# TensorE in two 64-row halves, the lower one lagging behind the upper, in the attention pairs 19 to 47

## The chip, the cores and the metric

The kernel runs on one core of a Trainium2 chip. The metric is the device time of one execution in microseconds. Three runs of the kernel before gave 401.55, 402.24 and 403.20 us; the median, 402.24 us, is the time before. The profile is of one execution of its own, with a span of 399.5 us from the first to the last instruction.

## The reference

Cosine attention is followed by a two-layer feed-forward block:

```python
q_n = q / (np.linalg.norm(q, axis=-1, keepdims=True) + 1e-06)      # q, k, v: 8 x 12 x 448 x 64
k_n = k / (np.linalg.norm(k, axis=-1, keepdims=True) + 1e-06)
scores = np.matmul(q_n, k_n.transpose(0, 1, 3, 2)) / tau
attn = softmax(scores)                                             # over the keys
x = (attn @ v).transpose(0, 2, 1, 3).reshape(3584, 768)
h = x @ w_in                                                       # 768 x 2048
g = h * np.clip(h + 3.0, 0.0, 6.0) / 6.0
out = g @ w_out                                                    # 2048 x 768
```

There are 8 batches of 12 heads, 448 tokens and 64 channels a head, in float32 in and out.

## The kernel before

The 96 heads are handled as 48 pairs, six pairs to a batch. Everything that TensorE multiplies is bf16, and everything it adds up lies in PSUM: two banks for the value products (PV, one for each head of a pair) and a ring of six banks (M0, M1, Y, Z, M2, M3) for all the rest.

For a pair, the queries and keys are loaded (`load_qk`), squared (`square`), reduced (`reduce`), turned into reciprocal norms on ScalarE (`norms`), normalised on GpSimd (`normalise`), transposed by a DMA (`crossbar`) into a tile tT, and the keys are copied into kz (`copy_k`) and km (`copy_k3`). Scores are computed with the keys on the partitions, in four groups. Groups 0 to 2 hold 128 keys of each head; the two heads lie on different 64 rows of TensorE's array, since a head has 64 channels. Group 3, "M", holds the last 64 keys of both heads in one matmul over all 128 rows, with the other quarters of km at zero. Each of the seven results takes a bank, and ScalarE turns it into exponentials (`exps`, L463) in a tile at. `values` (L486) multiplies them with the values, which have a column of ones, so that column 64 is the softmax's sum: 24 matmuls over 128 rows (groups 0 to 2) and 8 over 64 rows (group 3, four a head). `finish_values` (L506, L507) divides on VectorE, and `back_crossbar` or `back_two` transposes the result by a DMA into xT, of which there are two, one a batch.

The first layer (`mm1_unit`, L598) makes 128 of the 2048 features for a batch's 448 tokens with six matmuls of 448 columns in one bank. ScalarE makes the clipped factor (`relu`, L614) and VectorE the product g (L620); then the bank is free. `mm1_two` weaves two such units, so that the last of six matmuls of both comes at the end. The second layer works on pairs of 128-token blocks in Strassen-like form with seven products (`product_unit`, L794), named 1 to 7, eight matmuls of 384 columns each. VectorE makes the sums of g that they need (`g_sum`, L772). Products 2, 4, 5 and 3 are copied out by ScalarE (L813, L831, L842), products 1, 6 and 7 are added by VectorE (L819, L851), and GpSimd adds the parts up (L823 to L835). Products 6, 2 and 5 go on in the bank of 1, 4 and 3, after that bank was read, unless they are written as "5a" or "2a", with a bank of their own and an addition on GpSimd.

The order of the work is written out by hand. PLAN lists everything up to pair 17; then a loop makes one turn for each of the pairs 18 to 47, with the units of both layers that TURNS names for it (F is one first-layer unit, FF two woven ones, "4.3" product 4 of block pair 3, "+1.3" the sum for it) and sums on VectorE that `side` names. Instructions reach each engine's queue in this order and are executed in it. A turn of the kernel before starts with value group 3 of the pair before (64-row halves), the scores of groups 0 to 2 (64-row halves, in pairs), their exponentials, value groups 1 and 2 of the pair before, and its finish; then the units, with score group 3 behind the first; last, value group 0. After pair 47 the units of units[NP] finish the second half of the work without attention.

The functions that the change touches, and those that call them, with the profile's line numbers:

## Time and profile before

| | |
|---|---|
| median of three runs | 402.24 us (401.55 to 403.20) |
| profiled execution, span | 399.5 us |
| TensorE busy in the span | 391.4 us |
| VectorE, ScalarE, GpSimd busy | 291.1, 274.3, 235.9 us |
| granted TensorE clock, mean | 0.999 |
| turns 19 to 47, to the last value product (120.6 to 336.0 us) | 215.4 us |
| VectorE, ScalarE, GpSimd busy in them | 154.6, 154.6, 146.1 us |

The profile is a trace of every engine's instructions with their start and length, and of the semaphores that they wait for. Busy time is the union of an engine's instructions. A matmul's length is the time until its result is written, so that matmuls that follow each other closely overlap; the pace of TensorE is read from starts, not from lengths. "64*128" in a row is the rows and columns of the array that an instruction uses. A row of groups gives line, engine, operation, out<-in, shapes and count, then busy time and the mean length in ns, then the engine's idle time before it and what ended that.

### The profile page before, as it was taken

Reading aid. Unit: us, or ns where it says so; the run is one execution under the profiler, and the core shown is the slowest. Engines: PE = TensorE matmul, PEld = TensorE weight load, DVE = VectorE, ACT = ScalarE, POOL = GpSimd, SP = SyncE. Lnnn points to the kernel's source line nnn. Section 1 sums busy time; section 2 is a strip of 40 time slices with the busy share of each in tenths; the row PEclk is TensorE's granted clock in tenths of the full one; section 3 lists DMA queues with packets and bytes.
Section 4 is the critical chain, followed back from the end, with each engine's and each line's share of the span. In section 5 each row is a group of like instructions: output and inputs, shape, how many; then the busy total and the mean of one; then the engine's idle time right before and its main releaser. Section 6 shows DMA issues by size and latency. Waiting matters only on the chain.

```text
span 399.5 us, 9623 instructions
## 1 busy us (share of the span) xinstructions
PE 391.4 (98%) x3673; PEld 230.9 (58%) x3673; DVE 291.1 (73%) x514; ACT 274.3 (69%) x627; POOL 235.9 (59%) x234
## 2 busy tenths in 40 slices
PE   7999999999999999999999999999999999999996
PEld 5656466555555556555555555555565556555563
DVE  6898988889878597766878775976766565645663
ACT  6899998886887676887776776767658655224230
POOL 7897229652853989579859829688396500400070
PEclk9999999999999999999999999999999999999999
DMA  8999987797987678795888386694953424230133
GB/s 292 291 226 252 240 188 206 149 172 193 222 201 171 159 193 183 174 231 152 196 178 230 81 203 158 155 198 136 193 125 75 103 48 67 46 74 21 31 71 97
DMA packets 92365, 63.73 MB, mean 160 GB/s; under 512 B 56096, under 2 KB 91552, under 8 KB 92320
## 3 DMA queue, kind: packets, MB, share of 16 engines
q1 hardware_dynamic: 87408, 56.45, 58.6%
q0 software_dynamic: 4512, 6.29, 9.3%
q8 instruction: 28, 0.46, 0.5%
q10 hardware_dynamic: 400, 0.39, 0.3%
q14 instruction: 17, 0.14, 0.1%
HBM read 45.61 MB, written 11.01 MB: 142 GB/s over the span
## 4 chain that ended last, share of the span: by engine, by line
PE 90%; ACT 5%; DMA 1%; DVE 1%; POOL 1%; issue 0%; SPq 0%; ACTq 0%
PE M L598 24%; PE M L794 19%; PE PV L486 11%; PE Y L598 6%; PE Z L598 6%; PE M L445 5%; PE Z L794 5%; PE Y L794 4%; ACT at L463 4%; PE Z L445 1%; PE Y L445 1%; PE M L874 1%; PE PV L1016 1%; DMA big<-in_q_dram 1%; POOL nrm L297 1%; PE Z L659 1%
## 5 line engine op out<-in xcount | busy, mean ns | idle before, releaser
L598 PE MATMUL M<-xT,w_in_sb 128*128 128x448 bf16 x522 | 110.7, 353 | 0.1
L598 PEld LDWEIGHTS <-w_in_sb 128*128 128x128 bf16 x768 | 72.0, 98 | 62.2 <-issue 1.9
L463 ACT ACTIVATE at<-M 128x448 bf16<-128x448 f32 x192 | 96.4, 569 | 16.7 <-PE M L445 15.7
L297 POOL TENSOR_TENSOR nrm<-big,r 128x896 bf16<-128x896 f32 (+1 forms) x46 | 77.1, 1680 | 27.8 <-ACT r L260 10.7
L229 POOL TENSOR_TENSOR big<-big 128x896 f32<-128x896 f32 (+3 forms) x41 | 60.8, 1488 | 16.6 <-DVE n L241 11.0
L620 DVE SCALAR_TENSOR_TENSOR gT<-u,M 128x448 bf16<-128x448 bf16 x76 | 46.2, 616 | 32.0 <-ACT u L614 31.8
L614 ACT ACTIVATE u<-M 128x448 bf16<-128x448 f32 x87 | 48.5, 560 | 28.3 <-PE M L598 27.9
L486 PEld LDWEIGHTS <-at 128*128 128x128 bf16 (+1 forms) x1536 | 53.0, 97 | 22.8 <-issue 14.4
L486 PE MATMUL PV<-vx,at 128*128 128x65 bf16 (+1 forms) x1536 | 62.3, 193 | 0.3 <-DVE on L507 0.2
L241 DVE TENSOR_REDUCE n<-big 128x14 f32<-128x896 f32 (+1 forms) x50 | 51.7, 1041 | 5.7 <-POOL big L229 3.9
L794 PEld LDWEIGHTS <-gT 128*128 128x128 bf16 x336 | 32.5, 98 | 23.3 <-issue 0.4
L823 POOL TENSOR_TENSOR big<-big 128x384 f32<-128x384 f32 x13 | 13.4, 1034 | 53.7 <-ACT big L842 53.5
L794 PE MATMUL M<-w_out_sb,gT 128*128 128x384 bf16 x224 | 40.2, 326 | 0.0
L794 PEld LDWEIGHTS <-gs 128*128 128x128 bf16 x280 | 27.0, 98 | 18.7 <-issue 0.5
L402 POOL COPY km<-tT 64x128 bf16<-64x128 bf16 x34 | 14.0, 413 | 34.7 <-PE M L445 9.7
L507 DVE TENSOR_TENSOR on<-PV,rc 128x512 bf16<-128x512 f32 x48 | 33.2, 691 | 1.7
L794 PE MATMUL M<-w_sum,gs 128*128 128x384 bf16 (+1 forms) x192 | 34.2, 323 | 0.0
L463 ACT ACTIVATE at<-Y 128x448 bf16<-128x448 f32 x52 | 29.6, 569 | 6.0 <-PE Z L445 5.9
L445 PE MATMUL M<-tT,kz 64*128 64x448 bf16 x169 | 31.1, 351 | 0.3 <-DVE gT L620 0.2
L463 ACT ACTIVATE at<-Z 128x448 bf16<-128x448 f32 x50 | 28.8, 576 | 0.4 <-PE M L445 0.4
L598 PE MATMUL Y<-xT,w_in_sb 128*128 128x448 bf16 x126 | 27.4, 353 | 0.0
L316 POOL CAST vx<-big 128x512 bf16<-128x512 f32 x36 | 24.1, 672 | 4.9 <-DMA big<-in_v_dram 4.9
(137 smaller groups left out, 563.1 us busy)
## 6 DMA issues: line engine op xcount, KB each, us to landing
big<-in_k_dram SPq DMA_DIRECT2D x24, 448.0 KB, 4.5
big<-in_q_dram SPq DMA_DIRECT2D x24, 448.0 KB, 4.2
out_dram<-o SPq DMA_DIRECT2D x107, 96.0 KB, 2.2
big<-in_v_dram SPq DMA_DIRECT2D x48, 128.0 KB, 4.2
big<-in_v_dram SPq DMA_DIRECT2D x48, 96.0 KB, 4.1
w_out_sb<-in_moe_w_out_dram POOLq DMA_DIRECT2D x4, 768.0 KB, 9.4
w_in_sb<-in_moe_w_in_dram POOLq DMA_DIRECT2D x4, 384.0 KB, 10.7
w_in_sb<-in_moe_w_in_dram POOLq DMA_DIRECT2D x2, 768.0 KB, 21.5
```

The source lines that it names most:

```text
L229: engines[e].tensor_tensor(out=o, in0=i, in1=i, op=ALU.mult)
L241: nc.vector.tensor_reduce(out=n2s[d % 2][:, j % 2, c], in_=sq[:, :, :, :].rearrange("p g c d -> p (g c) d")[:, c, :], axis=AX.X, op=ALU.add,)
L297: engines[e].tensor_tensor(out=nrm[:, :, g, :].rearrange("p c g d -> p g c d"), in0=raw_of[j][:, g, :, :], in1=rs[d % 2][3][:, j % 2, :] . ...
L316: (engines[e].copy if e == "a" else engines[e].tensor_copy)(out=o, in_=f)
L445: nc.tensor.matmul(o, ks, qt[rows], start=True, stop=True)
L463: nc.scalar.activation(out=o, in_=x, func=AF.Exp, scale=inv_tau)
L486: nc.tensor.matmul(pv_out(j, h), at[rows, n, q_cols(i // HP, j)], vt[rows, 3 + h if name == "M" else 5 * h + int(name[1]), :], start=(name ...
L507: nc.vector.tensor_tensor(out=on[:, :, :, :].rearrange("p j h d -> p h j d"), in0=pv4[:, :, :, 0:D], in1=rc[:, :, :].to_broadcast([128, 2, ...
L598: nc.tensor.matmul(ps[:, 0:S], w_in_sb[:, cc, fc * 128 : (fc + 1) * 128], x[:, cc, 0:S], start=(cc == 0), stop=(cc == CC - 1),)
L614: nc.scalar.activation(out=u[:, :], in_=ps[:, 0:S], func=AF.Relu, bias=0.5, scale=1.0 / 6.0)
L620: nc.vector.scalar_tensor_tensor(out=g[:, fc, c0 : c0 + S], in0=u[:, :], scalar=1.0, in1=ps[:, 0:S], op0=ALU.min, op1=ALU.mult,)
L794: nc.tensor.matmul(m, lhs[:, c, :], rhs[:, c, c0 : c0 + width], start=(base is None and c == 0), stop=(c == KC - 1), skip_group_check=True,)
```

## The change

In pairs 19 to 47 (from value group 3 of pair 18 on), every matmul over 128 rows is replaced by two over 64 rows: an "upper" one over partitions 0 to 63, and a "lower" one over partitions 64 to 127 that adds to the same bank. The lower one is put into the program 1650 ns later, on a clock that counts columns / 2.4 + 2.3 ns for each upper one. Scores of groups 0 to 2 are 64-row matmuls as before; the first head's is an upper one, the second head's a lower one with a bank of its own. Where a bank goes from one half to the other, TensorE waits for the last matmul of the other half in that bank. Work on the other engines that belongs behind a product (exponentials, clipping, copies, sums, loads, transposes) is put into the program with the same delay. The bank for a new result is the one released longest ago, in the program's order, in place of a fixed turn of six. The scores of a pair are spread over the turn (group 0 at its start, 1 and M after the first unit, 2 after the second), value group 3 moves to the end of its own turn, and TURNS and `side` are written anew: product 1, 3 or 4 of a block pair mostly comes earlier in its turn, six "5a" become plain 5, and three sums for product 1 move from `side` into TURNS.

Cut to its core, with the unchanged parts of functions left out:

```diff
+    LAG = 1650.0
+    HALVES = (slice(0, 64), slice(64, 128))
+    lanes, later, clock = [], deque(), [0.0]
+    def half_product(h, key, out, lhs, rhs, start, stop):
+        if key in last_half and last_half[key][0] != h:
+            info = mybir.DependencyInfo(mybir.DependencyClass.Sync, mybir.DependencyReason.DATA)
+            wait = nc.tensor.nop(nofuse=True)
+            tc.add_manual_dep(wait.ins, last_half[key][1].ins.name, info, reason="one half of the array at a time in a bank")
+        ins = nc.tensor.matmul(out, lhs, rhs, start=start, stop=stop, skip_group_check=True)
+        last_half[key] = h, ins
+    def after(f, *args):
+        if lanes:
+            later.append((clock[0] + LAG, f, args))
+        else:
+            f(*args)
+    def catch_up(t):
+        while later and later[0][0] <= t:
+            _, f, args = later.popleft()
+            f(*args)
+    def upper(cols, *args):
+        catch_up(clock[0])
+        half_product(0, *args)
+        clock[0] += cols / 2.4 + 2.3
+    def lower(*args):
+        later.append((clock[0] + LAG, half_product, (1, *args)))
+    def accumulate(ops, done):
+        for key, out, lhs, rhs, start, stop in ops:
+            if not lanes:
+                nc.tensor.matmul(out, lhs, rhs, start=start, stop=stop, skip_group_check=True)
+                continue
+            (lhs0, rhs0), (lhs1, rhs1) = ((lhs[h], rhs[h]) for h in HALVES)
+            lower(key, out, lhs1, rhs1, False, stop)
+            upper(out.shape[-1], key, out, lhs0, rhs0, start, False)
+        after(done)
 
     def next_bank():
+        if lanes:
+            return min((x for x in ring if not unread.get(id(x))), key=lambda x: freed.get(id(x), -1))
         ring_n[0] += 1
         return ring[(ring_n[0] - 1) % len(ring)]
+    def release(key):
+        assert unread[key] > 0
+        unread[key] -= 1
+        if not unread[key]:
+            ring_n[1] += 1
+            freed[key] = ring_n[1]
+            last_half.pop(key, None)

...
+    def half_exps(i, g, h, o, key):
+        if (i, g) not in at_of:
+            m = len(GROUPS[g])
+            at_of[(i, g)] = ats[m][at_n[m] % len(ats[m])]
+            at_n[m] += 1
+        nc.scalar.activation(out=at_of[(i, g)][:, h, 0:S], in_=o, func=AF.Exp, scale=inv_tau)
+        release(key)
+    def lane_scores(i, g):
+        jq = i // 2 * 2 + (i >= XJ)
+        needs(("TR", jq), ("CS" if g == 3 else "CK", i), ("VA", i - 2, g))
+        qt = crossed(jq)[:, :, i % 2, :]
+        if g == 3:
+            o, key = bank_of(None, 1)
+            o, ks = o[:, 0:S], km[:, i % 2, :]
+            def done():
+                issued.update((("SC", i, 3), ("EX", i, 3)))
+                half_exps(i, 3, 0, o, key)
+            accumulate([(key, o, ks, qt, True, True)], done)
+            return
+        ks = kz[i % 2][:, 128 * g : 128 * g + 128]
+        def second():
+            o, key = bank_of(None, 1)
+            half_product(1, key, o[:, 0:S], ks[HALVES[1]], qt[HALVES[1]], True, True)
+            after_second.append((o[:, 0:S], key))
+        def done():
+            issued.update((("SC", i, g), ("EX", i, g)))
+            if g == 2:
+                issued.add(("SM", i))
+            half_exps(i, g, 1, *after_second.pop())
+        after_second = []
+        after(second)
+        o, key = bank_of(None, 1)
+        upper(S, key, o[:, 0:S], ks[HALVES[0]], qt[HALVES[0]], True, True)
+        half_exps(i, g, 0, o[:, 0:S], key)
+        after(done)
+    def lane_values(i, g):
+        needs(("VC", i), ("FI", i - 1), ("EX", i, g), *values_after(i, g))
+        at = at_of.pop((i, g))
+        vt = vx[i % NVX]
+        c = slice(0, 0)
+        if g == 3:
+            for j in range(4):
+                for h in range(2):
+                    args = (
+                        ("PV", h), pv_out(j, h), at[HALVES[h], 0, q_cols(i // HP, j)], vt[HALVES[h], 3 + h, :], False, False
+                    )
+                    if h:
+                        lower_args = args
+                    else:
+                        upper_args = args
+                lower(*lower_args)
+                upper(D + 1, *upper_args)
+            return
+        accumulate(
+            [
+                (
+                    ("PV", n), pv_out(j, n), at[:, n, q_cols(i // HP, j)], vt[:, 5 * n + g, :], g == 0 and j == 0, g == 2
+                )
+                for n in range(2)
+                for j in range(4)
+            ],
+            lambda: None,
+        )
+        issued.add(("VA", i, g))
+
...
-        def products_of(ccs):
-            for cc in ccs:
-                nc.tensor.matmul(
-                    ps[:, 0:S],
-                    w_in_sb[:, cc, fc * 128 : (fc + 1) * 128],
-                    x[:, cc, 0:S],
-                    start=(cc == 0),
-                    stop=(cc == CC - 1),
-                )
-
-        if ends is None:
-            products_of(range(CC))
-        else:
-            products_of(range(CC - 1))
-            ends.append(lambda: products_of([CC - 1]))
+        def products_of(ccs, done):
+            accumulate(
+                [
+                    (key, ps[:, 0:S], w_in_sb[:, cc, fc * 128 : (fc + 1) * 128], x[:, cc, 0:S], cc == 0, cc == CC - 1)
+                    for cc in ccs
+                ],
+                done,
+            )
...
+        def done():
+            post["a"].append(relu)
+            if lanes:
+                finish_all()
+        if ends is None:
+            products_of(range(CC), done)
+        else:
+            products_of(range(CC - 1), lambda: None)
+            ends.append(lambda: products_of([CC - 1], done))
...
-        for c in range(KC):
-            nc.tensor.matmul(
-                m,
-                lhs[:, c, :],
-                rhs[:, c, c0 : c0 + width],
-                start=(base is None and c == 0),
-                stop=(c == KC - 1),
-                skip_group_check=True,
-            )
+        assert base is None or (n, base) in ready
...
-        post["a" if name in "2345" else "v"].append(finish)
+        def ended():
+            post["a" if name in "2345" else "v"].append(finish)
+            if lanes:
+                finish_all()
+        accumulate(
+            [
+                (key, m, lhs[:, c, :], rhs[:, c, c0 : c0 + width], base is None and c == 0, c == KC - 1)
+                for c in range(KC)
+            ],
+            ended,
+        )
...
-        20: "F F 1.0 F 6.0",
-        21: "F F 3.1 F 5.1",
-        22: "F F 4.1 F 2.1 +1.1",
-        23: "F 1.1 F 6.1",
+        20: "F 1.0 F F 6.0",
+        21: "F 3.1 F F 5.1",
+        22: "F 4.1 F +1.1 F 2.1",
+        23: "1.1 F F 6.1",
         24: "F F 7.0",
         25: "FF F 3.2",
-        26: "F F F 5a.2",
-        27: "F 4.2 F 2.2",
-        28: "F 1.2 F 6.2",
+        26: "F 5.2 F F",
+        27: "4.2 F F 2.2",
+        28: "1.2 F F 6.2",
         29: "F F F 7.1",
         30: "F F F 7.2",
-        31: "3.3 F F F 5a.3",
-        32: "F F 4.3 F 2.3",
-        33: "F F 1.3 F 6.3",
+        31: "3.3 F F F 5.3",
+        32: "F 4.3 F +1.3 F 2.3",
+        33: "F 1.3 F F 6.3",
         34: "F F 7.3 +75.4 F 3.4",
-        35: "F 5a.4 4.4 F 2.4",
-        36: "F 1.4 F 6.4",
+        35: "4.4 F 5.4 F 2.4",
+        36: "1.4 F F 6.4",
         37: "7.4 +75.5 F F F 3.5",
-        38: "F F 5a.5 4.5 F 2.5",
-        39: "F F 1.5 F 6.5",
-        40: "F F 7.5 +75.6 3.6 F 5a.6",
-        41: "F 4.6 F 2.6",
-        42: "F 1.6 F 6.6 7.6",
-        43: "3.7 F F F 5a.7",
-        44: "F F 4.7 F 2.7",
-        45: "F F 1.7 F 6.7",
-        46: "F F 3.8 F 5.8",
+        38: "F 5.5 4.5 F +1.5 F 2.5",
+        39: "F 1.5 F F 6.5",
+        40: "F F 7.5 +75.6 F 3.6",
+        41: "4.6 F 5.6 F 2.6",
+        42: "1.6 F F 6.6 7.6",
+        43: "3.7 F F F 5.7",
+        44: "F 4.7 F +1.7 F 2.7",
+        45: "F 1.7 F F 6.7",
+        46: "F 3.8 F F 5.8",
         47: "F 7.7 F",
     }
...
-        27: sums(2, "621"),
+        26: sums(2, "62"),
+        27: sums(2, "1"),
         28: [(g_left, 2)],
         29: [(keep, 2, 0)],
         30: [(keep, 2, 1)],
         31: sums(3, "75"),
         32: sums(3, "62"),
-        33: sums(3, "1"),
         35: sums(4, "621"),
         37: [(g_left, 4)],
         38: sums(5, "62"),
-        39: sums(5, "1"),
         41: sums(6, "621"),
         43: sums(7, "75"),
         44: sums(7, "62"),
-        45: sums(7, "1"),
...
+    def turn(i):
+        stream.extend(units[i])
         n_u = len(stream)
         even = i % 2 == 0
 
         def prepare(*what):
             for op, n, *args in what:
                 if n < (NP // 2 if op in ("NO", "LV") else NP):
-                    do(op, n, *args)
-
-        if i > FIRST:
-            do("VA", i - 1, 3)
-        for g in range(3):
-            do("SC", i, g)
-        for g in range(3):
-            do("EX", i, g)
-        for g in range(1, 4):
-            if ("VA", i - 1, g) not in issued:
-                do("VA", i - 1, g)
-        do("FI", i - 1)
+                    after(do, op, n, *args)
+        lane_scores(i, 0)
+        lane_values(i - 1, 1)
+        lane_values(i - 1, 2)
+        after(do, "FI", i - 1)
         for f, *args in side.get(i, []):
-            f(*args)
-
+            after(f, *args)
         if (i - 1) % HP > 3:
-            do("XB", i - 1)
+            after(do, "XB", i - 1)
         elif even:
-            do("XP", i - 2)
-        if i == FIRST:
-            do("LQ", i + 6)
+            after(do, "XP", i - 2)
         if even:
             prepare(("XD", i + 2))
         if i % HP == 0 and i > FIRST:
             prepare(("LV", (i + 4) // 2))
-        do("UU", 1)
-        do("SC", i, 3)
-        do("EX", i, 3)
+        unit()
+        lane_scores(i, 1)
+        lane_scores(i, 3)
         if not even:
             prepare(("CS", i + 1))
         prepare(("SQ", i + 5, "p", 0, 7))
-        do("UU", 1)
-        n = 2
         if not even:
-            prepare(("NO", (i + 3) // 2))
-            if n_u > 3 and stream[0][0] is product_unit and units[i][1][0] is mm1_unit:
-                do("UU", 1)
-                n += 1
-            prepare(("CK", i + 1), ("CK", i + 2))
-        do("UU", n_u - n - 1)
+            prepare(("CK", i + 1))
+        unit()
+        lane_scores(i, 2)
+        if not even:
+            prepare(("NO", (i + 3) // 2), ("CK", i + 2))
+        while len(stream) > 1:
+            unit()
         if i != FIRST + 1:
             prepare(("NM", i + 3, "p"), ("VC", i + 2, "p"))
         if even:
             prepare(("XD", i + 3))
-        do("UU", 1)
+        unit()
         if i == FIRST + 1:
-            while post["p"]:
-                finish_units("p")
+            after(finish_all, "p")
             prepare(("NM", i + 3, "p"), ("VC", i + 2, "p"))
         prepare(("RE", i + 5), ("LQ", i + 7))
         if i % HP != HP - 1 and not even:
             prepare(("LV", (i + 5) // 2))
-        while post["p"]:
-            finish_units("p")
-        do("VA", i, 0)
-    do("VA", NP - 1, 3)
-    do("VA", NP - 1, 1)
-    do("VA", NP - 1, 2)
+        after(finish_all, "p")
+        lane_values(i, 0)
+        lane_values(i, 3)
+        issued.add(("VA", i, 3))
+
...
+    lanes.append(True)
+    lane_values(FIRST, 3)
+    issued.add(("VA", FIRST, 3))
+    for i in range(FIRST + 1, NP):
+        turn(i)
+    lane_values(NP - 1, 1)
+    lane_values(NP - 1, 2)
+    catch_up(clock[0] + 2 * LAG)
+    lanes.clear()
```

More of the change, by code (lines that the diff above doesn't have):

```diff
@@ L1 @@
+from collections import deque
 from contextlib import ExitStack
@@ L398, in copy_k3 @@
             assert i % 2 == 0
-            needs(("SM", i - 1))
+            needs(("SC", i - 1, 3))
             for g in range(2):
@@ L822, in both @@
         def both():
+            ready.add((n, "both"))
             nc.gpsimd.tensor_tensor(out=e, in0=d, in1=e, op=ALU.add)
@@ L850, in finish @@
             elif name == "1":
+                assert (n, "both") in ready
                 nc.vector.tensor_tensor(out=d, in0=m, in1=d, op=ALU.add)
             elif name == "6":
+                assert (n, "rest") in ready
                 added(1, RIGHT, e)
             else:
+                assert (n, "1") in ready
                 added(0, LEFT, d)
@@ L1028, in unit, with finish_all @@
         f, *args = stream.pop(0)
-        f(*args)
+        if f in (mm1_unit, mm1_two, product_unit, single_unit, mm2_unit):
+            f(*args)
+        else:
+            after(f, *args)
+    def finish_all(engines="av"):
+        for e in engines:
+            while post[e]:
+                finish_units(e)
     def finish_units(e):
@@ L1036, in whole_units @@
             unit()
-            for e in engines:
-                while post[e]:
-                    finish_units(e)
+            if not lanes:
+                finish_all(engines)
     OPS = {
@@ L1086 @@
         run(line)
-    for i in range(FIRST, NP):
-        assert not stream
-        stream = list(units[i])
+    def turn(i):
+        stream.extend(units[i])
         n_u = len(stream)
```

44 lines of the change are left out of this document (35 added, 9 removed).

## Prediction

> **What bounds the kernel now.** I read the page first, then the busy time of the stretch that the change touches, then who waited in it, then TensorE's order of work in one turn. The page:
>
> ```profile
> span 399.5 us, 9623 instructions
> PE 391.4 (98%) x3673; PEld 230.9 (58%) x3673; DVE 291.1 (73%) x514; ACT 274.3 (69%) x627; POOL 235.9 (59%) x234
> ...
> PE   7999999999999999999999999999999999999996
> ...
> PEclk9999999999999999999999999999999999999999
> ...
> PE 90%; ACT 5%; DMA 1%; DVE 1%; POOL 1%; issue 0%; SPq 0%; ACTq 0%
> ```
>
> TensorE never stops, at full clock, and the chain that ends last lies on it for 90%. The busy time from turn 19 to the last value product of pair 47:
>
> ```profile
> 120.60:336.00 215.40, 215.40 (x2077) 126.65 (x2074) 154.61 (x261) 154.58 (x366) 146.14 (x139) 1.00 0.68 156
> ```
>
> PE is busy for 215.40 of 215.40 us; VectorE and ScalarE have 154.6 each (72%), GpSimd 146.1 (68%). So a gain must come from TensorE's own stream. What a busy PE hides shows in the waits of the weight loads in this stretch (engine, line, releaser: us in all, times, longest):
>
> ```profile
> PEld L486 <- issue: 9.0, 29, 0.4
> PEld L794 <- DVE gT L772: 0.3, 1, 0.3
> PEld L794 <- issue: 0.2, 1, 0.2
> ```
>
> Nothing else holds TensorE up, but 29 times, once a pair, the load for a value product starts late without a releaser. The order of work shows where (start, us to the end of the last, count):
>
> ```profile
> 249.48 0.63 PE L486 MATMUL PV<-vx,at 128*128 128x65 bf16 x16
> 249.95 0.54 PE L445 MATMUL M<-tT,kz 64*128 64x448 bf16 x3
> 250.14 0.35 PE L445 MATMUL Y<-tT,kz 64*128 64x448 bf16 x1
> 250.35 0.35 PE L445 MATMUL Z<-tT,kz 64*128 64x448 bf16 x1
> 250.35 0.36 PE L445 MATMUL M<-tT,kz 64*128 64x448 bf16 x1
> 250.65 0.67 PE L486 MATMUL PV<-vx,at 128*128 128x65 bf16 x16
> 251.15 1.46 PE L794 MATMUL M<-w_sum,gs 128*128 128x384 bf16 x8
> 252.45 0.35 PE L445 MATMUL M<-tT,km 128*128 128x448 bf16 x1
> 252.64 1.30 PE L598 MATMUL M<-xT,w_in_sb 128*128 128x448 bf16 x6
> 253.77 1.30 PE L598 MATMUL Y<-xT,w_in_sb 128*128 128x448 bf16 x6
> 254.91 0.35 PE L598 MATMUL Z<-xT,w_in_sb 128*128 128x448 bf16 x1
> ```
>
> and, from the same view begun a little later, where the first row stands apart by its rows of the array:
>
> ```profile
> 249.82 0.29 PE L486 MATMUL PV<-vx,at 64*128 64x65 bf16 x8
> ```
>
> Six 448-wide matmuls take 254.91 - 253.77 = 1.14 us, 189 ns each; a product's eight 384-wide ones 252.45 - 251.15 = 1.30, 162.5 each; sixteen 65-wide ones 251.15 - 250.65 = 0.50, 31 each (29.4 by the width's share). Two 64-row halves on different rows run as one: the two scores at 250.35 stand side by side. The last scores start at 250.35 and the next full matmul at 250.65: 0.30, not 0.19, so 0.10 to 0.11 is lost on the way back to full rows. On the way in, eight value products from 249.48 to 249.82 take 0.34, not 0.24: 0.10 again. I take 0.097 for each, 5.6 us in 29 turns.
>
> **The change, part by part.**
>
> *The stream.* Counted in the changed program, the uppers from pair 18's last value product to pair 47's are 468 matmuls of 448 (first layer), 448 of 384, 116 scores of 448 and 832 of 65: 468 x 0.189 + 448 x 0.1625 + 116 x 0.189 + 832 x 0.0294 = 207.6 us (207.5 before rounding). The lowers make the same stream 1.65 us later, so the end comes at 209.2; one change of rows in and one out, 0.2. Against 215.3 that is **-5.95 us**. LAG is a product's 8 x 0.1625 and the 0.326 that one lasts (PE rows below), so it is paid once, not per turn.
>
> *Value products at 31 instead of 29.4 ns.* The excess of 1.5 ns comes in both lanes, now at different times: 832 x 1.5 ns is 1.2 us if only one lane's shows, 2.4 if both. I take **+1.8**.
>
> *Waits for banks.* A bank that a first-layer product (or any full-row unit) fills is now held 1.65 us longer, and every turn still needs seven banks for scores out of the six. In the trace TensorE starts its matmuls in program order, so I take it that one that waits for a bank holds both halves and all that is queued behind it. The prices of giving a bank back:
>
> ```profile
> L614 ACT ACTIVATE u<-M 128x448 bf16<-128x448 f32 x52 | 29.6, 571 | 14.1 <-PE M L598 13.9
> L620 DVE SCALAR_TENSOR_TENSOR gT<-u,M 128x448 bf16<-128x448 bf16 x52 | 31.9, 617 | 24.9 <-ACT u L614 24.8
> L506 DVE RECIPROCAL rc<-PV 128x8 f32<-128x8 f32 x29 | 6.0, 206 | 13.5 <-PE PV L486 12.8
> L507 DVE TENSOR_TENSOR on<-PV,rc 128x512 bf16<-128x512 f32 x29 | 20.0, 691 | 1.0
> L772 DVE TENSOR_TENSOR gs<-gT 128x1024 bf16<-128x1024 bf16 x23 | 19.6, 853 | 0.0
> L772 DVE TENSOR_TENSOR gT<-gT 128x1024 bf16<-128x1024 bf16 x17 | 16.6, 979 | 0.6
> L463 ACT ACTIVATE at<-M 128x448 bf16<-128x448 f32 x134 | 67.1, 569 | 13.1 <-PE M L445 12.1 <-PE Y L445 0.5
> L842 ACT COPY big<-M 128x384 f32<-128x384 f32 x10 | 4.8, 482 | 3.8 <-PE M L794 3.8
> L598 PE MATMUL M<-xT,w_in_sb 128*128 128x448 bf16 x312 | 67.0, 352 | 0.0
> L794 PE MATMUL M<-w_sum,gs 128*128 128x384 bf16 x152 | 27.6, 326 | 0.0
> ```
>
> After a first-layer stream: 0.163 until the last matmul has ended (352 less 189), 0.571 ScalarE, 0.617 VectorE: 1.35 us with no queue. After an upper score 0.352 + 0.569 = 0.92, after a product that ScalarE copies 0.65. The time allowed is what TensorE's order leaves: the uppers between the bank's last upper and its next user, less 1.65 where that user is an upper.
>
> - Turns 19 and 25 (two first-layer products woven together). Both give their banks back late and nearly at once, with only 0.41 and 0.24 us of uppers until one is wanted. In turn 25 that lacks 1.35 - 0.24 = 1.1; in turn 19 VectorE also has the pair's finish (0.206 + 0.691) and three sums ahead, 1.2 to 1.9. I take 1.2 + 1.5: **+2.7**. Before, the same pair had a ring of banks without lag, and no wait.
> - Turns 21, 22, 26, 32, 44, 46: uppers between are score, score, product, score, first-layer unit, 3 x 0.189 + 1.30 + 1.13 = 3.00 (or the like), less 1.65 = 1.35, just the price without a queue; but VectorE first has finish and two sums, 0.90 + 0.85 + 0.98 = 2.73 from the end of the value products, 1.13 us before the stream's end. So the bank comes about 2.73 - 1.13 + 0.62 = 2.2 late against 1.35 allowed less the 0.16 of draining already counted: 1.0 short, 0.5 where the sums go at their fastest, 0 if they overlap. I take 0.6: **+3.6**.
> - Turns 20, 33, 39, 45 and 19 again: the same 1.35 without sums; 0.1 each for the wake-ups, **+0.5**.
> - A product on a bank that must be read first (6 on 1, 2 on 4, 5 on 3): 0.81 allowed in ten turns, 0.62 in turn 38, against 0.65 for ScalarE's copy and 0.72 for VectorE's sum: **+0.6**, up to 3 with a queue.
> - Lower scores with 1.35 to 1.5 (turns 31, 34, 35, 40, 41, 43): price 0.73 plus one other ScalarE instruction, **+0.5**.
>
> Turns 23, 24, 27 to 30, 36, 37, 42, 47 have 1.7 us or more for most reuses, and I charge nothing.
>
> *The waits between halves.* The built program has 243 new waits in TensorE's queue. A product's first lower waits for its last upper, done 8 x 0.1625 + 0.163 = 1.46 us after the start; due at 1.65, so 0.19 is left to load and start, and others have more. I take 0. The nearest row is the sync queue's:
>
> ```profile
> L538 SPq EVENT_SEMAPHORE  x12: 17/17/17, 116.0 to 336.1; - x12
> ```
>
> 243 x 17 ns is 4.1 us where nothing covers them; behind each stand the next uppers.
>
> *Moved work.* Finishing, sums, normalising, casts, loads and transposes are issued 1.65 us later on VectorE, GpSimd and SP, by the same counts except six GpSimd additions of about 1.0 us that go. I charge nothing: most have a turn of over 5 us in hand. The tightest is the transpose of pair 23 before turn 25's first-layer product:
>
> ```profile
> xT<-on SPq DMA_TRANSPOSE x25, 3.5
> ```
>
> With the reduction and finish ahead it lands about 0.2 us before the sixth matmul needs it; 0.6 late at worst.
>
> **Sum:** -5.95 + 1.8 + 2.7 + 3.6 + 0.5 + 0.6 + 0.5 = **+3.75**. The profiled span of 399.5 goes to 403.3; the median of the runs is 402.24, 2.7 above this span, which I keep: **406.0 us**.
>
> **Order of endings.** A rule weighs against the change. In the trace paired halves have equal length, start 0.00 apart and so end together; no row shows a short matmul beside a long one. The Trainium skill, "TensorE: Matmul & The Clock Gate", Part 3 on packing small matmuls, says that matmuls start and end in program order. Were a short one to keep its rows until the other half's long one ends, the sum would be that of the third rival; by the rows I take it that only equal speed counts.
>
> **Rivals.**
> 1. *The banks come in time* (the other sign): VectorE's and ScalarE's queues are short, since spread scores leave no burst, and each wait shifts the next. For it: both engines are idle for 28% of the stretch. Against it: the 0.24 us. With all waits gone but 1.2 us of value excess: 402.24 - 5.95 + 1.2 = 397.5; it decides for faster as long as waits stay under 2.7 us. With the woven pairs alone, 399.6.
> 2. *The halves disturb each other.* In the rows of 249.82 and 249.95 four pairs of halves take 0.13 us, not 0.118: 3 ns a pair. On some 1,030 long matmuls in two lanes, 3 to 6 ns each are 6 to 12 us, or the waits between halves show (4.1): 409 to 418.
> 3. *It does not overlap when staggered.* Each of the 28 short matmuls of a pair takes the neighbour's 189 in place of 29: 160 ns x 28 x 29 = 130 us in one lane, 532 us; one half after the other altogether, 207 more, 609. The side-by-side scores speak against it.
>
> **How the numbers follow.** About 0.5% (2 us) can be told from no change in this kernel: below 400.2 is faster, above 404.3 slower. The forecast, waits of 5 to 12 us (403 to 409), 0.53; rival 1, 397.5 to 400.5, 0.24; rival 2, 0.16; rival 3, 0.05 (by the order of endings alone, 0.03); the switches gained and something else lost for no change, 0.02. Faster: most of rival 1, 0.22. Same: its rest (0.02), the last 0.02 and 0.12 of the forecast, 0.16. Slower 0.62. The range takes in rival 1 and most of rival 2: 397.5 to 414; the forecast's own is 402 to 410.
>
> **What will show it.** In the changed profile: the 29 late weight loads at L486 gone (else step 1 is wrong); waits of TensorE for VectorE's gT and ScalarE's at, over 1 us in turns 19 and 25 and near 0.5 in the six turns with sums; first-layer uppers 189 ns apart with lowers between them. Wrong if PE has no such waits (then near 397.5), if uppers come at over 195 ns (rival 2), or if VectorE's queue makes the waits of 0.81 us turn by turn, which would put it near 410.

## The result and the profile after

The changed kernel takes 424.41 us (median of four runs, 423.00 to 428.33); the kernel before took 402.47 us beside it (four runs, 401.55 to 403.20). The ratio is 1.056, with a 95% interval of 1.051 to 1.062: it is slower by some 22 us. The prediction was 406.0 us, in a range up to 414.0. The sign was right, the size far off.

The page of the changed kernel, in the same rows as those shown of before:

```profile
span 421.5 us, 13180 instructions
PE 395.3 (94%) x5330; PEld 273.5 (65%) x5330; DVE 293.1 (70%) x514; ACT 278.3 (66%) x627; POOL 228.8 (54%) x228
...
PE   7999999999999889779997999979999999999996
...
PEclk9999999999999999999999999989999999999999
...
PE 74%; DVE 12%; ACT 7%; POOL 3%; issue 2%; DMA 1%; ACTq 0%; DVEq 0%; POOLq 0%
```

The row of TensorE has dips now, and one slice has a lower granted clock. The other engines have about as much work as before, but VectorE's share of the chain that ends last has gone from 1% to 12%. The stretch with the halves, whole (start and end, length, then busy us and count for TensorE, its loads, VectorE, ScalarE and GpSimd, then clock and DMA):

```profile
120.70:358.10 237.40, 219.09 (x3738) 169.31 (x3737) 156.70 (x261) 158.61 (x366) 140.01 (x133) 0.99 0.69 143
```

It lasts 237.4 us in place of 215.4: all of the 22 us are here. TensorE, which was busy for 215.40 of 215.40 us, is now idle for 18.3. Who it waited for (releaser: us in all, times, longest):

```profile
PE M L174 <- DVE gT L744: 8.3, 9, 2.1
PE Y L174 <- DVE gT L744: 3.0, 2, 1.9
PE Z L174 <- DVE gT L744: 2.7, 1, 2.7
PE PV L174 <- ACT at L528: 1.1, 4, 0.3
PE Y L174 <- DMA xT<-on: 1.0, 1, 1.0
PE M L174 <- DVE big L979: 0.9, 1, 0.9
PE M L174 <- issue: 0.7, 1, 0.7
```

14.0 of these us are waits for gT, VectorE's product behind the first layer, which gives a bank back. A wait of this view begins only when the last matmul's length is over. The loss of pace is larger, so I worked it out from the starts and widths of the 3,728 matmuls on halves (ten full ones lie at the window's edges). From the first to the last half 236.9 us pass. The upper stream needs 207.5 of them and the lag 1.65; 24.3 are stops, in which neither half goes on, and 3.5 are a slower pace between stops.

The longest stop, in turn 38, shows what a stop is made of. First VectorE, then GpSimd, then TensorE, each in order of time (start, length, engine, line):

```profile
274.12 0.69 DVE L638 TENSOR_TENSOR on<-PV,rc 128x512 bf16<-128x512 f32 x1
274.73 1.70 DVE L905 TENSOR_TENSOR gs<-gT 128x1024 bf16<-128x1024 bf16 x1
...
276.46 2.06 DVE L905 TENSOR_TENSOR gT<-gT 128x1024 bf16<-128x1024 bf16 x1
278.45 0.60 DVE L744 SCALAR_TENSOR_TENSOR gT<-u,Z 128x448 bf16<-128x448 bf16 x1
```

```profile
274.20 1.68 POOL L287 TENSOR_TENSOR big<-big 128x896 f32<-128x896 f32 x1 [0.78 <-DVE rc L637]
275.84 2.14 POOL L355 TENSOR_TENSOR nrm<-big,r 128x896 bf16<-128x896 f32 x1
```

```profile
275.26 1.17 PE L174 MATMUL M<-w_out_sb,gT 64*128 64x384 bf16 x12
279.11 0.35 PE L174 MATMUL Z<-xT,w_in_sb 64*128 64x448 bf16 x1 [2.67 <-DVE gT L744]
```

TensorE wants bank Z and gets it 0.06 us after VectorE's product is done. That product stands behind two sums (L905), and the two take 3.76 us together, although one lasts 0.69 at its fastest. Each ends 0.55 us after a GpSimd instruction that ran beside it: square ends at 275.88 and the sum at 276.43; normalise ends at 277.98 and the sum at 278.52. So the sums wait for GpSimd, and TensorE for the sums. The Trainium skill has this rule, "SBUF — State Buffer", section "Who interferes with whom": a VectorE instruction with two inputs in SBUF and a GpSimd instruction that reads SBUF exclude each other, and whichever comes second is blocked until the first has finished. The rows agree.

It was so before the change too. VectorE and GpSimd of the kernel before, at 214 us:

```profile
213.97 1.26 DVE L772 TENSOR_TENSOR gs<-gT 128x1024 bf16<-128x1024 bf16 x1
215.26 2.06 DVE L772 TENSOR_TENSOR gT<-gT 128x1024 bf16<-128x1024 bf16 x1
```

```profile
213.00 1.68 POOL L229 TENSOR_TENSOR big<-big 128x896 f32<-128x896 f32 x1
214.63 2.14 POOL L297 TENSOR_TENSOR nrm<-big,r 128x896 bf16<-128x896 f32 x1
```

The ends are 0.55 us apart here too (214.68 and 215.23; 216.77 and 217.32), and TensorE did not stop. Sums of the same lengths stood there before; the order has lost the room for them. By cause, the 24.3 us of stops are:

| place | us | the prediction's term |
|---|---|---|
| turns 21, 22, 26, 32, 44, 46, VectorE's sums ahead of a product | 1.57, 1.97, 2.06, 2.30, 1.09, 0.61 = 9.6 | 3.6 |
| turn 38, likewise | 2.8 | none |
| banks of the woven units in turns 19 and 25 | 0.88 + 1.30 = 2.2 | 2.7 |
| transpose of xT, turn 25 | 1.1 | 0, at worst 0.6 |
| one half waiting for the other in a bank, woven units in turns 19 and 25 | 0.32 + 0.31 + 0.31 = 0.9 | 0 |
| lower scores, eight places | 2.0 | 0.5 |
| exponentials that value products wait for | 1.9 | none |
| product 6 on the bank of 1, turn 28 | 1.1 | 0.05 (0.6 in all) |
| no releaser, turn 43 to 44 | 0.87 | none |
| turns 20, 33, 39, 45 | 0.4 | 0.5 with turn 19 |
| changes of rows, the lower clock behind turn 38 (see the end) and small ones | 1.4 | 0.2 |

### The profile page after: what moved, and what is told of

Read it like the earlier page. It is cut to its first block, busy times and chain, and to the rows that moved or that the text cites. A ratio compares the mean times of both kernels' runs of the same rounds, so it can differ in the third digit from the quotient of the medians.

```text
span 421.5 us, 13180 instructions
## 1 busy us (share of the span) xinstructions
PE 395.3 (94%) x5330; PEld 273.5 (65%) x5330; DVE 293.1 (70%) x514; ACT 278.3 (66%) x627; POOL 228.8 (54%) x228
## 4 chain that ended last, share of the span: by engine, by line
PE 74%; DVE 12%; ACT 7%; POOL 3%; issue 2%; DMA 1%; ACTq 0%; DVEq 0%; POOLq 0%
PE M L174 19%; PE M L201 16%; PE PV L174 7%; PE Z L174 6%; PE Y L174 4%; PE PV L617 4%; PE Z L201 4%; PE Y L201 3%; DVE gT L905 3%; DVE gT L744 3%; PE PV L1155 2%; ACT at L521 2%; ACT at L528 2%; DVE gs L905 2%; DVE on L638 2%
## 5 line engine op out<-in xcount | busy, mean ns | idle before, releaser
L174 PE MATMUL M<-xT,w_in_sb 64*128 64x448 bf16 x600 | 122.1, 351 | 7.8 <-DVE gT L744 7.5
L174 PEld LDWEIGHTS <-w_in_sb 64*128 64x128 bf16 x936 | 78.4, 94 | 21.0 <-issue 8.2
L174 PE MATMUL PV<-vx,at 64*128 64x65 bf16 x1664 | 70.6, 190 | 1.1 <-ACT at L528 1.1
L174 PEld LDWEIGHTS <-at 64*128 64x128 bf16 x1664 | 64.0, 94 | 11.3 <-ACT at L528 2.0
L287 POOL TENSOR_TENSOR big<-big 128x896 f32<-128x896 f32 (+3 forms) x41 | 60.8, 1488 | 14.5 <-DVE n L299 10.6
L174 PE MATMUL M<-w_sum,gs 64*128 64x384 bf16 x352 | 64.5, 322 | 1.7 <-DVE big L979 0.9
L174 PEld LDWEIGHTS <-gT 64*128 64x128 bf16 x480 | 42.5, 94 | 23.6 <-issue 17.2
L174 PE MATMUL M<-w_out_sb,gT 64*128 64x384 bf16 x304 | 56.3, 327 | 0.0
L201 PEld LDWEIGHTS <-w_in_sb 128*128 128x128 bf16 x300 | 28.0, 98 | 25.4 <-issue 1.9
L174 PE MATMUL Z<-xT,w_in_sb 64*128 64x448 bf16 x180 | 40.1, 356 | 2.7 <-DVE gT L744 2.7
L201 PE MATMUL M<-xT,w_in_sb 128*128 128x448 bf16 x204 | 42.4, 353 | 0.1
```

The source lines that it names most:

```text
L174: ins = nc.tensor.matmul(out, lhs, rhs, start=start, stop=stop, skip_group_check=True)
L201: nc.tensor.matmul(out, lhs, rhs, start=start, stop=stop, skip_group_check=True)
L287: engines[e].tensor_tensor(out=o, in0=i, in1=i, op=ALU.mult)
```

## The experiments

Beside these runs the kernel before took 402.62 us (median of seven). Each experiment but "Earlier sums" was run once. The changed kernel's own four runs spread over 5 us (423.00 to 428.33), so a difference of 2 or 3 us in time says little by itself; there the stops in the trace decide. "Stops" are worked out as above. The letters in the expectations stand for these theories: A, banks come late because of VectorE's queue, with its sums in it (A1: because GpSimd lengthens them); B, the halves themselves cost the time, whatever the other engines do; C, the new order alone makes the stops, with the lag or without; D, the halves wait for each other; F, TensorE waits for its own instructions.

**No sums.** VectorE's sums are left out in the turns with halves.

```diff
-        nc.vector.tensor_tensor(out=o[:, :, :], in0=x, in1=y, op=op)
+        if not lanes:
+            nc.vector.tensor_tensor(out=o[:, :, :], in0=x, in1=y, op=op)
```

> Leaves out VectorE's sums of g in pairs 19 to 47 (the seven-product blocks then multiply unsummed blocks). Theory A, that the sums stand ahead of the first-layer product that gives a bank back: TensorE's waits in turns 21, 22, 26, 32, 38, 44 and 46 (1.57 + 1.97 + 2.06 + 2.30 + 2.83 + 1.09 + 0.61 = 12.4 us in the changed profile) go, and with them the slower clock behind the longest: 11 to 13.5 us less, 411 to 413.5. Theory B, that the staggered halves and the waits between them cost the time: at most 3 us less, 421 or more.

Measured: 410.35 us, 14.1 less; stops 11.6 in place of 24.3, pace excess 2.95. The waits of TensorE:

```profile
PE M L174 <- DVE gT L744: 1.4, 4, 0.7
...
PE Y L174 <- DVE gT L744: 1.1, 1, 1.1
```

The waits for gT fall from 14.0 to 2.5 us. Of the 22 us, 14 hang on the sums.

**Light GpSimd.** The sums stay; square and normalise take one of seven columns in these turns.

```diff
+            if lanes:
+                o, i = o[:, :, 0:1, :], i[:, :, 0:1, :]
...
+        w = 1 if lanes else 7
-            out=nrm[:, :, g, :].rearrange("p c g d -> p g c d"),
+            out=nrm[:, 0:w, g, :].rearrange("p c g d -> p g c d"),
```

> GpSimd squares and normalises one seventh of its columns in pairs 19 to 47 (the rest keeps old values); the sums stay. Theory A1, that an in-place sum lasts 2.06 us instead of 0.69 because GpSimd's long instructions run beside it: sums are all near 0.69, the waits of turns 22, 26, 32 and 38 shrink by 1.37 each, 5 to 7 us less, 417 to 419.5. Theory A2, that the sums' place in the queue alone matters, or B: within 1.5 us of 424.4.

Measured: 413.84 us, 10.6 less; stops 15.1. The stops in the seven turns with sums go from 12.4 to 5.0, turn 38's from 2.83 to 0.48. The group of the sums into gT, in the changed kernel and in this one:

```profile
L905 DVE TENSOR_TENSOR gT<-gT 128x1024 bf16<-128x1024 bf16 x17 | 19.0, 1119 | 0.5
```

```profile
L908 DVE TENSOR_TENSOR gT<-gT 128x1024 bf16<-128x1024 bf16 x19 | 14.4, 757 | 0.6
```

The second row takes in two sums from outside these turns; the 17 inside have a mean of 725 in place of 1,119 ns. That is three quarters of the gain of leaving the sums out (10.6 of 14.1). So it is GpSimd's work beside the sums that makes most of the stops. The step is larger than expected: besides the 7.4 us in the seven turns, the stop in turn 28 (1.1, there VectorE itself waits for GpSimd) and the lower clock behind turn 38 are gone. With every sum short, the seven turns still lose 5.0.

**Lanes alone.** No sums, light GpSimd, and the clipping and the product g on 64 of 448 columns, so that a bank comes back soon.

```diff
-                out=u[:, :], in_=ps[:, 0:S], func=AF.Relu, bias=0.5, scale=1.0 / 6.0
+                out=u[:, 0:w], in_=ps[:, 0:w], func=AF.Relu, bias=0.5, scale=1.0 / 6.0
...
-                out=g[:, fc, c0 : c0 + S],
-                in0=u[:, :],
+                out=g[:, fc, c0 : c0 + w],
+                in0=u[:, 0:w],
```

> In pairs 19 to 47 no sums, GpSimd's two long instructions on one seventh, and clipping and product of the first layer on 64 of 448 columns: banks come back at once, TensorE's order is that of the change. Theory A: the stream at its own pace, 402.2 - 5.95 + 1.2 to 3.5 for value products in two lanes, with late transposes and exponentials (2 to 4 us) still in it: 398 to 403. Theory B: the two lanes still lose, 409 or more.

Measured: 409.0 us, not 398 to 403. The waits, and a window's clock (the third figure from the end):

```profile
PE Y L174 <- DMA xT<-on: 2.9, 1, 2.9
PE M L174 <- issue: 1.3, 1, 1.3
```

```profile
171.00:175.00 4.00, 3.89 (x20) 0.50 0.86 181
```

No wait for VectorE is among the large ones. In their place stands the transpose before turn 25's first-layer product, 3.03 us. Around it TensorE's clock is 0.50 for 6.8 us (169.6 to 176.5), which costs some 3 us more. A stop of 1.42 has no releaser. The pace excess is 2.9, and twice in the woven units one half waits for the other (0.31 and 0.49). B's number came, but only this and the pace belong to the halves; the rest lies in stops of other causes. "Lanes alone, earlier sums' order" below takes most of them away.

**Earlier sums.** All of the computation. The sums go behind score group M, some a turn earlier, and the woven units are dissolved.

```diff
-        19: "FF 5a.0 F 2a.0",
+        19: "5a.0 F F F 2a.0",
-        25: "FF F 3.2",
+        25: "3.2 F F F",
...
-        21: sums(1, "75"),
-        22: sums(1, "62"),
+        20: sums(1, "75"),
+        21: sums(1, "62"),
-        37: [(g_left, 4)],
-        38: sums(5, "62"),
+        37: [(g_left, 4)] + sums(5, "62"),
-        46: sums(8, "75"),
-        47: sums(8, "62"),
+        45: sums(8, "75"),
+        46: sums(8, "62"),
...
-        for f, *args in side.get(i, []):
-            after(f, *args)
         if (i - 1) % HP > 3:
...
         lane_scores(i, 3)
+        for f, *args in side.get(i, []):
+            after(f, *args)
```

> The whole computation. The sums are issued behind score group M instead of behind the pair's finish, some a turn earlier, so that they fall between two first-layer products on VectorE; the woven pairs of turns 19 and 25 become single units behind a product. Theory A: the 12.4 us of waits in the sum turns fall to about 2, the woven pairs' 2.2 and the late transposes' 2.0 go: 12 to 15 us less, 409.5 to 412.5. Theory B: at most 4 us less, 420 or more.

Measured: 414.53 us (four runs, 414.10 to 415.38), 9.9 less than the changed kernel and 1.028 of before (1.022 to 1.034). Stops 15.2. The largest waits:

```profile
PE M L174 <- DVE big L979: 2.3, 2, 1.6
PE M L174 <- DVE gT L744: 1.9, 1, 1.9
PE M L174 <- DVE gT L905: 1.8, 2, 1.1
```

The order on VectorE and of the units is worth about 10 us without leaving anything out. Two things were changed at once and not run apart: in turns 19 and 25, where the woven units were, the stops fall from 4.2 to 2.1; the other 7 us of stops went where the sums moved. What is late next is product 1's own sum (L979), on which product 6 waits for its bank, 3.7 us of stops in three turns. In two of them (1.71 and 0.96) it stands behind the moved sums; in the third (turn 28, 1.05) it waits for GpSimd's addition, as in the changed kernel.

**Lag of 1,500 ns**, in place of 1,650 (`LAG = 1500.0`).

> The change with LAG 1500 instead of 1650, the whole computation. Theory A, that a bank held longer is what TensorE waits for: each of some 30 waits for a bank is 0.15 us shorter and the drain too, 3 to 6 us less than 424.4; lower products start 0.04 us before their wait would matter at 1.46 us. Theory D, that 1650 is the least that the waits between halves bear: these waits show in TensorE's records and the time does not fall.

Measured: 422.17 us, 2.2 less, which one run does not tell from the changed kernel's spread. In the trace stops fall by 3.3 to 21.0, but the pace excess rises from 3.5 to 6.2. Banks that come 0.15 us sooner help A's stops. Gaps of about 0.13 us now stand in many products, which fits lower halves waiting for uppers, that is D; the records do not name them. At 1,650 D shows only in the woven units, 0.9 us.

**Order only.** The new order, full 128-row matmuls and no lag; only the scores of groups 0 to 2 and value group 3 are pairs of halves, as before.

```diff
-    LAG = 1650.0
+    LAG = 0.0
...
-            if not lanes:
-                nc.tensor.matmul(out, lhs, rhs, start=start, stop=stop, skip_group_check=True)
-                continue
+            if lanes:
+                catch_up(clock[0])
+                clock[0] += out.shape[-1] / 2.4 + 2.3
+            nc.tensor.matmul(out, lhs, rhs, start=start, stop=stop, skip_group_check=True)
+            continue
```

> The changed order of units, scores, sums and banks, with no lag and full 128-row matmuls (scores of groups 0 to 2 and value group 3 as 64-row pairs side by side). Three stretches of 64 rows a turn instead of one, so 58 changes there and back more, 58 x 0.195 = 11.3 us. Theory A, that the lag's longer hold of the banks makes the waits: 413.5 with at most 3 us of waits, 412.5 to 417, and the late changes of rows themselves visible. Theory C, that the new order and the choice of the bank released longest ago make them: 10 us or more of waits for VectorE, 424 or more.

Measured: 421.56 us, between the two. TensorE's waits for VectorE, and those of its loads at changes of rows:

```profile
PE Z L174 <- DVE gT L746: 2.8, 2, 1.6
PE M L174 <- DVE gT L746: 2.4, 3, 1.4
PE Y L174 <- DVE gT L746: 2.0, 3, 1.2
```

```profile
PEld L203 <- issue: 17.1, 84, 0.2
```

Without the lag this order changes rows three times a turn in place of once: 58 more changes there and back at 2 x 0.097 are 11.3 us. Worked out from starts, 8.5 us of stops are waits for VectorE. With 402.2 that gives 422.0. So the order alone makes 8.5 us of such waits, though its changes of rows leave VectorE 11 us more time; in the changed kernel, where a bank is held 1.65 us longer, they come to 16.1 (12.4 with sums, 2.2, 1.1 and 0.4 in the table). C and A both hold in part: with the lag the waits are nearly twice those of the order.

**Lanes alone, earlier sums' order.** The two kernels together (sums and most of GpSimd's, the clipping's and the product's columns left out).

> Like lanes_alone (no sums, short GpSimd, short clipping and product), with the order of slots (no woven pairs, first-layer units behind a product in turns 19 and 25). Theory A: the transpose's wait of 3.0 us in turn 25 and the slower clock behind it (together about 5 us) go: 403 to 405 with what is left (a fetch of instructions, value products, some waits for exponentials). Theory B, a cost of the lanes that no wait shows: 408 or more.

Measured: 402.97 us, no different from before. Its stretch:

```profile
120.40:337.40 217.00, 213.64 (x3736) 171.94 (x3732) 91.70 (x219) 137.70 (x366) 69.38 (x133) 1.00 0.74 157
```

Stops 5.3, pace excess 2.3. Without the stops it would be 397.7, near the first rival's 397.5. The stretch would then be 211.7 us, 3.7 shorter than before, where the prediction had 4.15 (5.95 less 1.8). So even with two fifths of VectorE's and half of GpSimd's load gone (91.7 and 69.4 us of busy time in place of 156.7 and 140.0), the stops that are left use up the gain. The best version that computes everything, earlier sums, is 2.8% slower than the kernel before.

**Shifted instructions.** 64 one-column matmuls ahead of the first half move all later instructions by their number.

```diff
+    for _ in range(64):
+        nc.tensor.matmul(PV[:, 0, 260:261], ident[:, :], ident[:, 0:1], start=False, stop=False, skip_group_check=True)
     lanes.append(True)
```

> The change with 64 one-column matmuls (128 more instructions for TensorE, about 1.9 us) ahead of the first halves. Theory F, that the stop of 0.9 us without a releaser at the first matmuls of a product in turn 43 or 44 is a late fetch of instructions: it leaves that product, and stands some 130 instructions earlier or elsewhere or not at all. Rival: a wait that the records don't name: it stays at the same product. Time 425 to 427.

Measured: 427.7 us, and the stop without a releaser in turn 43 to 44 is gone. F said so, but F would also have allowed a stop elsewhere; and with a lag of 1,500 ns the stop there is down to 0.17 us without any shift. The stronger evidence is the order of events: in six runs with such a stop in turn 43 to 44 (of 0.7 to 1.4 us) TensorE went on 1.26 to 1.38 us after a packet of its instruction queue had landed (here: landed at 310.63, on at 311.89). The queue, before and after:

```profile
q8 instruction: 28, 0.46, 0.5%
```

```profile
q8 instruction: 42, 0.69, 0.7%
```

TensorE's 3,673 matmuls became 5,330, and 14 more packets of 16 KB come. The timing supports F; that a late packet is the cause is not shown.

## Why the prediction was wrong, and where it was right

- **The step that failed: turns with sums, +3.6.** It measured 9.6, and 2.8 more in turn 38, which was missing from the list though it has two sums like the six. The mechanism was right: the product that frees a bank stands behind finish and two sums on VectorE. The step that was mis-sized is VectorE's queue: the sums were put in with the mean lengths of their groups, 0.85 and 0.98, and with only the finish ahead of them. A mean hid two kinds of sum. The same sum's rows by line, shapes apart (least, middle, greatest length in ns), before and after:

```profile
L772 DVE TENSOR_TENSOR gT<-gT x21: 684/693/2061, 77.2 to 344.9; 128x1024 bf16<-128x1024 bf16 x21
```

```profile
L905 DVE TENSOR_TENSOR gT<-gT x21: 681/693/2061, 77.6 to 366.9; 128x1024 bf16<-128x1024 bf16 x21
```

  Half of them last 0.69, but some three times as long, when GpSimd squares or normalises beside them. Turns 22, 26, 32 and 38 meet one of 2.05 or 2.06 each, turn 38 one of 1.70 too (3.76 us for its two sums and not 1.83): these four stops are 9.2 of the 12.4. Turn 46 has two short sums and stops for 0.61, just the 0.6 charged. The spread stood in the first row before the change, and the experiment with light GpSimd shows that it decides. Turn 21 shows another omission. Its sums are short, but the pair's reduction, which the sum left out, stands ahead of the finish, so that the finish starts 0.93 us after the value products' end (140.62):

```profile
140.54 1.08 DVE L299 TENSOR_REDUCE n<-big 128x14 f32<-128x896 f32 x1 [0.30 <-POOL big L287]
```

  The argument "0.5 where the sums go at their fastest" took one bound alone; the one at their slowest was left out.
- **Moved work, 0, transposes 0.6 late at worst.** The one in turn 25 cost 1.1 us; 0.3 of it would have been a wait for the other half anyway. The step left out the sync queue, which VectorE's later finish now meets with other work in it (time, length, queue):

```profile
166.11 1.12 SPq L780 DMA_DIRECT2D out_dram<-o  x2
167.28 0.59 SPq L256 DMA_DIRECT2D big<-in_k_dram  x1
167.97 1.22 SPq L669 DMA_TRANSPOSE xT<-on  x1
```

  Two stores and a load go ahead; the transpose starts at 167.97 and lands at 173.45, 5.5 us and not the 3.5 of the row used. In the experiment with lanes alone this one wait was 3.03.
- **Waits between halves, 0.** For products and for units that are not woven no such stop shows. In a woven unit the sixth upper comes after only two lowers, so the bank goes to the other half three times. Turn 19, where the transpose had landed at 123.72:

```profile
123.98 0.35 PE L174 MATMUL M<-xT,w_in_sb 64*128 64x448 bf16 x1 [0.16 <-PE M L174]
124.48 0.35 PE L174 MATMUL M<-xT,w_in_sb 64*128 64x448 bf16 x1
```

  The upper waits for the lower before it, the next lower for the upper: stops of 0.32 and 0.31. Turn 25 has one more of 0.31 behind its transpose. With shifted instructions, where that transpose came in time, turn 25 has two of 0.31.
- **Lower scores, 0.5, and product on a read bank, 0.6.** They measured 2.0 and at least 1.1. The four longest of the lower scores' stops (0.26 to 0.49) end with VectorE's product on a bank, which the price of a ScalarE instruction did not have; in turn 28 VectorE's sum first waits 0.89 us for GpSimd's addition. The exponentials that value products wait for (1.9) were not charged at all, and 0.87 without a releaser could not be seen before.
- **Right: the stream, -5.95.** The 29 late loads of the changes of rows are gone; two changes are left, of 0.097 us each. The lanes do overlap at full pace when staggered, and the third rival falls. TensorE in turn 43, both halves in one view:

```profile
310.45 0.35 PE L174 MATMUL Z<-tT,kz 64*128 64x448 bf16 x1
310.59 0.22 PE L174 MATMUL PV<-vx,at 64*128 64x65 bf16 x2
310.64 0.35 PE L174 MATMUL M<-tT,km 64*128 64x448 bf16 x1
310.65 0.31 PE L174 MATMUL PV<-vx,at 64*128 64x65 bf16 x5
310.81 0.32 PE L174 MATMUL M<-w_sum,gs 64*128 64x384 bf16 x1
310.83 0.35 PE L174 MATMUL M<-xT,w_in_sb 64*128 64x448 bf16 x1
311.89 0.33 PE L174 MATMUL M<-w_sum,gs 64*128 64x384 bf16 x1 [0.71 <-issue]
```

  One half starts 448-wide matmuls at 310.45, 310.64 and 310.83, 189 ns apart. Beside it the other runs seven 65-wide ones from 310.59 to 310.81, 31 ns each, and none waits for the long one's end. (The last row is the stop without a releaser.) The rule of the Trainium skill ("TensorE: Matmul & The Clock Gate", Part 3), that matmuls start and end in program order, holds here for the signals of their ends and not for their starts. The halves' 656 signals, taken in program order, each come 13 to 91 ns after the last end of all matmuls ahead of them, the other half's included. But 365 of the 3,728 start before a matmul of the other half that stands ahead of them in the program, by up to 0.55 us. So the prediction's premise of starts in program order was not quite right, and the order of ends costs time only where something waits for a signal: in turn 19 the lower had ended at 123.57, and its signal came at 123.85, behind an upper's end.
- **Right: woven pairs, 2.7, measured 2.2; turns without sums, 0.1 each, measured 0.05 to 0.1.** Where no sum stood ahead, the sum of drain, ScalarE and VectorE (1.35) held to a tenth.
- **Nearly right: value products at 31 ns, +1.8.** The pace between stops cost 3.5, with part of the lower clock behind turn 38 in it. Without sums and with light GpSimd, where the clock stayed up, it cost 2.95 and 2.9. This speaks against the second rival, which wanted 6 to 12.
- **The first rival** (banks in time) came out in no kernel. The one nearest to it computes no sums and leaves out much of VectorE's and GpSimd's work, and there 5.3 us of other stops stand on top of its 397.5.
- **Two small figures** of the working do not come out: 65 columns at the pace of 448 are 27.4 ns, not 29.4 (which is nevertheless the trace's own: most value products start 29 ns apart), and 397.5 with the woven pairs' 2.7 is 400.2, not 399.6. Neither moves the forecast.

Together: the prediction's waits and pace came to 9.7 us (2.7 + 3.6 + 0.5 + 0.6 + 0.5 + 1.8) and measured 27.8 less the 0.2 of the two changes of rows. The 18 us between are its miss (421.5 against 403.3); half of it, 8.8, is the turns with sums.

## What to carry to other kernels

Before an order is made tighter, read the lengths of the instructions that will stand on the path one by one or as least, middle and greatest, not as a mean: a mean of 0.98 us was mostly 0.69 and sometimes 2.06, and the long ones were those beside another engine's work. An engine that never stops hides how little room the others have; a change that holds each buffer longer spends that room everywhere at once, and 5.95 us of saved switches paid for less than a quarter of the stops. When a wait is costed at its price "without a queue", walk through each queue that the releaser sits in, the DMA queue too, and take the slow bound for the forecast where several such waits follow each other.

## What was not expected of the hardware

- VectorE's sum of two bf16 tiles takes 0.69 us alone and, in these turns, up to 2.06 beside GpSimd's square or normalise. All 17 sums of over 0.9 us in the stretch, eight before and nine after, end 0.54 or 0.55 us after a GpSimd instruction: a square, a normalise, an addition or a cast.
- After a stop of 2.83 us TensorE's granted clock went to 0.50. The windows of the changed kernel behind turn 38 (start and end, length, TensorE's busy time and count, clock, DMA):

```profile
279.00:281.00 2.00, 1.89 (x19) 0.86 0.66 146
281.00:283.00 2.00, 2.00 (x14) 0.50 0.72 160
283.00:285.00 2.00, 2.00 (x33) 0.79 0.24 53
```

  A share of 0.86 is 0.56 us at half clock in two, one of 0.79 is 0.84. So the lower clock begins 1.3 us after the work has begun again (279.1) and lasts 3.4 us. Around the stop of 3.03 us in lanes alone it begins before the work does and lasts 6.8. The Trainium skill, "TensorE: Matmul & The Clock Gate", Part 1, gives an idle window of about 3.4 us for that. The lengths, 3.4 and twice 3.4, agree with such a window; but stops of 2.83 and 3.03 us were enough here. The 64 one-column matmuls of the last experiment were followed by a clock of 0.50 too, for 6.8 us from 124.0 on, though TensorE had work.
- A stop of 0.7 to 1.4 us without a releaser, in turn 43 to 44 of each of six runs, close behind a packet of the instruction queue.
- A matmul on one half of the array can start up to 0.55 us before one on the other half that stands ahead of it in the program, while the signals of their ends keep the program's order.
